# State products behind the outputs' products of the pair in front, and one place for product 7

## The chip, the cores and the metric

The kernel runs on one core of a Trainium2 chip. The metric is the device time of that core in microseconds (us), the median of several executions. A core has five engines with instruction queues of their own: TensorE (PE, the matmuls), VectorE (DVE), ScalarE (ACT), GpSimd (POOL) and SyncE (SP, which here only issues DMAs). Each runs its own queue in program order and waits for another engine through semaphores.

## The reference

Two blocks follow one another. The first is a Mamba-2 scan over 4 sequences, 8 heads, 768 tokens, head size 32, state size 16: with decays `a`, inputs `x`, and `B`, `C`, chunk by chunk

```python
M = einsum('bhin,bhjn->bhij', Cc, Bc) * exp(cum[i] - cum[j]) * causal   # gram times decays
y = einsum('bhij,bhjd->bhid', M, xc) + einsum('bhin,bhnd->bhid', Cc, state) * exp(cum)
state = exp(sum(la)) * state + sum_j(B_j * x_j * exp(cum_end - cum_j))
```

The second takes y as 3072 tokens of 256 features: `h = y @ w_in` (2048 wide), `g = max(h, 0) + alpha * min(h, 0)` (PReLU), `out = g @ w_out`. Everything is float32.

## The kernel before

**Tiles.** A chunk has 128 tokens here; a *pair* is two chunks, so there are 12 pairs, three for each sequence. A *group* is two pairs, 512 tokens, so there are 6 groups. While group g runs through the second block, the two pairs of group g + 1 are prepared by the first block. Groups 1 to 5 do the second block's two products in a Strassen-like scheme (seven products of half-size blocks in place of eight); group 0 does them directly.

**A quad.** `quad(g, z, after)` handles a quarter (z = 0 to 3) of the hidden features of a group. On TensorE it makes seven products into two banks of PSUM, A and Y, through `first` (L770). The ones that matter here, in order: `first(A, …, t3)`, `first(Y, …, b22)`, `first(A, …, t4)`, `first(Y, …, b21)`. What leaves the banks: `c22` (VectorE, L793), the copy of `m1` into Y (ScalarE, L799), and `prelu` for g12, g22, g21 and g11, each with two multiplications by ScalarE (L753) and two by VectorE (L755). g21 comes from A after `t4`, and g11 from Y after `b21`. Banks A and Y are taken from a pool with two of them (`ps_h`), which the *gram* of a pair (below) uses as well, through `spare()`.

**The order of the work** is written out by hand. `quad` calls `after(1)` to `after(14)` at fourteen places between its own steps. `after` issues there:
- `product(g, z, n)`, n = 1 to 7 (L745): the output products of the *quad in front*, by the table `with_gram` in the even quads (z = 0, 2) of groups 1 to 4, and by `without` elsewhere. The tables differ in product 7 alone: place 11 in the one, place 9 in the other. Product 6 is at place 13, product 4 at place 14.
- `ssm(gp, n)`: n further stages of the generator `pair(gp)`, by the table `steps`.
- `pair_loads(gp)` (L385, GpSimd): B times its decays, tile `bn`, which the state products read; and, in quad (3, 7), `token_sums` for the next group (L725).
- parts of `combine` and `finish`, which end the group in front, and sums of weights in group 1.

**A pair of groups 2 to 5** (pairs 4 to 11; `fine` in the code) has these stages: the transposes of B and C (L469); four stages of decays (VectorE scans, L438); the state products `added` (L519, tile shape 128x64) with the update of the state `states` (VectorE L531, GpSimd L534) and `c_decayed` (GpSimd L487); the gram `products_bc` (L569, four row groups of 32 rows each, two in tiles of `ps_s`, two in `spare()` banks, the fourth in the one that Y had) and its product with the decays (VectorE L604), in two stages; and the outputs' products (L620 from the state, shape 64x128, and L627 from the chunk, shape 128x32) with their copies to `xT` (ScalarE, L634). The state products of a pair stand in an even quad at place 9, its gram at place 13 of the same quad, its outputs' products at place 5 of the odd quad behind. The two pairs of a group take one even and one odd quad each. The last pair of each sequence (5, 8, 11) needs the state of one chunk only, so it has half the state products.

A float32 matmul shows as two TensorE instructions in the trace.

Of the kernel before, what the change touches and what calls it, by code (L numbers as in the profile page):

```python
# [9 lines left out]
F32 = mybir.dt.float32  # L10
U32 = mybir.dt.uint32
U16 = mybir.dt.uint16
ALU = mybir.AluOpType
# [9 lines left out]
def kernel(  # L23
# [25 lines left out]
    nc = tc.nc  # L49
# [6 lines left out]
    P = 128  # L56
    Q = 128
# [6 lines left out]
    KC = d_model // P  # L64
# [44 lines left out]
    def ss_tile():  # L109
        if early[0] is None:  # L110
            return ps_s.tile([P, 512], F32, name="ss")
        early[0] += 1
        i = early[0] % (3 if ident_p else 4)
        return ps_s.tile([P, 512], F32, name="ss") if i < 2 else bank(i)
# [211 lines left out]
    held = {}  # L326
    bns = {}

    def identity_bank():


        m5_bank.append(bank(3))
        nc.scalar.copy(out=m5_bank[0][:, HT:], in_=ident_h[:, :HT])
        ident_p.append(m5_bank[0][:, HT:])
# [42 lines left out]
    def pair_loads(gp):  # L377

        b, c = divmod(2 * gp, CPB)
        nat, abc, xt, ap = loads["p", gp]  # L380

        bn = work.tile([P, 2, H * N], F32, name="bn")
        i, bi = divmod(b, 2)
        pj = prt[i].rearrange("p (b h c) -> p b c h", b=2, h=H)[:, bi, c : c + 2]
        nc.gpsimd.tensor_tensor(  # L385
            out=bn.rearrange("p k (h n) -> p k h n", h=H),
            in0=nat[:, 0].rearrange("p k (h n) -> p k h n", h=H),
            in1=pj.unsqueeze(3).to_broadcast([P, 2, H, N]), op=ALU.mult)
        return bn
# [22 lines left out]
    def spare():  # L412

        return ps_h.tile([P, GT], F32, name="hp", tag="hp")

    def pair(gp):

        b, c = divmod(2 * gp, CPB)
        nat, abc, xt, ap = loads["p", gp]
        last = c + 2 == CPB  # L420
        dec = work.tile([P, 2, H, Q], F32, name="dec")
        dv = dec.rearrange("p k h t -> p k (h t)")

# [37 lines left out]
            yield  # L461


        tp = spare() if gp == 1 else ss_tile()
        if gp == 0:
            keep_warm(tp, 3, Q)
# [20 lines left out]
            nc.gpsimd.tensor_tensor(out=cd.rearrange("p k t -> p (k t)"), in0=ct, in1=pf,  # L487
                                    op=ALU.mult)

        fine = gp >= 2 * GC // 2  # L490
        if gp < 2:
            spread_c()
        if gp == 0:
# [1 line left out]
            dps = spare()  # L495
            keep_warm(dps, 6, Q)
            yield
        bn = bns.pop(gp) if gp in bns else pair_loads(gp)
        if gp == 1:
            c_decayed()  # L500
            dps = spare()
# [1 line left out]
        elif gp:  # L503
            yield

        nk = 1 if last else 2
        st = [masked.get(b)]  # L510
        new = work.tile([P, 2, P], F32, name="state")
        sm = work.tile([P, 2, P], F32, name="sm")

        def added(dps):
            dps = dps.rearrange("p (k m) -> p k m", m=P)
            for k in range(nk):
                for w in range(KC):
                    ws = slice(64 * w, 64 * w + 64)
                    nc.tensor.matmul(dps[ws, k], bn[:, k, ws], xt[:, k, w * P : (w + 1) * P],  # L519
                                     start=True, stop=True, tile_position=(0, 64 * w),  # L520
                                     skip_group_check=True)
            return dps

        def states(dps):
            for k in range(nk):
                old = state.get(b)
                if old is None:
                    nc.scalar.copy(out=new[:, k], in_=dps[:, k])
                else:
                    e = (k + 1) * Q - 1  # L530
                    nc.vector.scalar_tensor_tensor(out=new[:, k], in0=old, scalar=pf[:, e : e + 1],  # L531
                                                   in1=dps[:, k], op0=ALU.mult, op1=ALU.add)
                state[b] = new[:, k]
            nc.gpsimd.tensor_tensor(out=sm[:, :nk], in0=new[:, :nk],  # L534
                                    in1=hmask.unsqueeze(1).to_broadcast([P, nk, P]), op=ALU.mult)
            st.extend(sm[:, k] for k in range(nk))
            masked[b] = st[-1]

        if fine:
            for k in range(2):  # L540
                for w in range(2):
                    half_decays(k, w)
                    if k == 1 and w == 1:
                        spread_c()
                    yield
        else:
            if gp > 1:
                states(added(ss_tile()))
                c_decayed()
            decays(0)  # L550
            if gp == 1:
                dps = added(dps)
            if gp:
                yield
            if gp != 1:
                decays(1)
            if gp > 1:
                spread_c()
# [24 lines left out]
        if gp == 0:  # L583
            gram = products_bc()
            dps = added(dps)
            yield
            c_decayed()
            times(dec[:, :, :2], one_less(gram))
        elif gp == 1:
            decays(1)  # L590
            gram = products_bc()
            g0 = one_less(gram)
            states(dps)
            times(dec[:, :, :2], g0)
        else:
            if fine:
                states(added(ss_tile()))
                c_decayed()
            yield
            gram = products_bc()  # L600
        for i, r in enumerate(r for r in ((2, 3, 0, 1) if fine else (3, 2, 1, 0) if gp > 1 else range(4))
                              if r in gram):
# [6 lines left out]
        yield  # L609


        y = [ss_tile()[:, : 2 * Q].rearrange("p (k t) -> p k t", k=2) for w in range(KC)]
        if gp < 2:
            keep_warm(y[0].rearrange("p k t -> p (k t)"), 2 - gp)
        begun = False
# [7 lines left out]
        for k in range(2):  # L623
            for w in range(KC):
                for q in range(4):
                    h = 4 * w + q
                    nc.tensor.matmul(y[w][32 * q : 32 * q + 32, k], xt[:, k, h * D : (h + 1) * D],  # L627
                                     dec[:, k, h], start=False, stop=True,
                                     tile_position=(0, 32 * q), skip_group_check=True)
        g, q = divmod(2 * gp, GC)  # L630
        if q == 0:
            xts[g] = xtp.tile([P, KC, GT], F32, name="xT")
# [342 lines left out]
    for f in range(FIRST, NF):  # L975
        if f in (5, 10):
            load_pair(3 + f // 10)
        if f == 5:
            load_rows(1)
        hidden(0, f)  # L980
        if f <= 10:
            ssm(2)
        if f >= 9:
            ssm(3)
        if f < FIRST + 2:
            convert_a(*pieces[f + 1 + (f > FIRST)])
        convert_next(first=f > FIRST)
        if f == FIRST:
            convert_a(*pieces[6])
        if f == 8:  # L990
            bns[3] = pair_loads(3)
        if f == 8:
            rows_clamp(1)
            held["pr"] = rows_scan(1)
            rows_out(1)
        output(f - FIRST)
        if f in in_steps:
            weight_sums(wi, in_sums, 0, in_steps[f])
    early[0] = None
    token_sums(1)  # L1000
    ssm(2 * GC // 2, 2)


    steps = {(0, 1): 0, (0, 2): 0, (0, 5): 0, (0, 9): 0, (0, 13): 0, (1, 1): 0, (1, 5): 0,
             (1, 12): 1, (1, 14): 1, (2, 1): 1, (2, 2): 1, (2, 5): 1, (2, 9): 1, (2, 13): 1,
             (3, 1): 1, (3, 5): 1, (3, 12): 2, (3, 14): 2}

    late_sums = {(0, 2): ((wqt, out_sums, 0, 0),), (0, 4): ((wqt, out_sums, 0, 1),),
# [6 lines left out]
    last_out = {3: ((0, 0),), 5: ((1, 0),), 7: ((2, 0),), 8: ((3, 0),), 11: ((0, 1),), 13: ((1, 1),),  # L1015
            14: ((2, 1), (3, 1))}

    with_gram = {3: 1, 5: 2, 7: 3, 8: 5, 11: 7, 13: 6, 14: 4}
    without = {3: 1, 5: 2, 7: 3, 8: 5, 9: 7, 13: 6, 14: 4}
    for i in range(NZ * (NG - 1)):  # L1020
        g, z = divmod(NZ + i, NZ)
        nxt = 2 * g + 2

        def after(j, g=g, z=z, i=i, nxt=nxt):
            places = with_gram if nxt < NP and z % 2 == 0 else without
            if i and j in places:
                product(*divmod(NZ + i - 1, NZ), places[j])
            if i == 0:
                for f, half in last_out.get(j, ()):
                    output(NF - LATE + f, half)  # L1030
            if (i, j) in ((0, 13), (1, 8)):
                store_first(i)
            for args in late_sums.get((i, j), ()):
                weight_sums(*args)
            if g > 1 and z == 0 and j in (5, 9, 13, 14):
                if j == 5:
                    comb[0] = combine(g - 1)
                next(comb[0], None)
            if g > 1 and z in (1, 3) and j == 11:
                finish(g - 1, z // 2)  # L1040
            if nxt + steps.get((z, j), NP) < NP:
                ssm(nxt + steps[z, j])
            if nxt < NP and (z, j) == (3, 7):
                token_sums(g + 1)
            ahead = nxt + {(1, 3): 1, (3, 8): 2}.get((z, j), NP)
            if ahead < NP:
                if ahead == 6:
                    rows_turn(1, held["pr"])
                bns[ahead] = pair_loads(ahead)

        comb = [None] if i == 0 else comb
        if z == 0 and nxt < NP:
            load_pair(nxt + 1)
        if z == 2 and nxt + 2 < NP:
            load_pair(nxt + 2)
        quad(g, z, after)
# [31 lines left out]
```

## Time and profile before

| what | value |
|---|---|
| time, median of 3 runs | 374.32 us (374.3 to 375.46) |
| span of the profiled execution | 372.9 us |
| TensorE busy | 365.1 us (98%) |
| VectorE, ScalarE, GpSimd busy | 243.9, 179.4, 201.1 us |
| granted TensorE clock | 0.998 |
| matmul instructions, L745 (output products) | 560, 140.8 us |
| L770 (`first`) | 560, 146.3 us |
| L569 (gram), all | 192, 31.6 us |
| L519 (state products), all | 80, 7.0 us |
| L620 and L627 (outputs' products), all | 464, 25.3 us |

The page gives busy time for each engine, the span in slices, the chain of work that ended last, and the costliest groups of instructions, with the idle time ahead of them and the instruction that ended it. A TensorE row's length is modelled, so lengths of neighbouring rows overlap; times between the *starts* of rows are what was measured. The timeline lists rows in order of time: start, length, engine, line, operation, output and inputs, shapes, and how many like rows were merged.

### The profile page before, as it was taken

Reading aid. Unit: us, or ns where it says so; the run is one execution under the profiler, and the core shown is the slowest. Engines: PE = TensorE matmul, PEld = TensorE weight load, DVE = VectorE, ACT = ScalarE, POOL = GpSimd, SP = SyncE. Lnnn points to the kernel's source line nnn. Section 1 sums busy time; section 2 is a strip of 40 time slices with the busy share of each in tenths; the row PEclk is TensorE's granted clock in tenths of the full one; section 3 lists DMA queues with packets and bytes.
Section 4 is the critical chain, followed back from the end, with each engine's and each line's share of the span. In section 5 each row is a group of like instructions: output and inputs, shape, how many; then the busy total and the mean of one; then the engine's idle time right before and its main releaser. Section 6 shows DMA issues by size and latency. Waiting matters only on the chain.

```text
span 372.9 us, 6183 instructions
## 1 busy us (share of the span) xinstructions
PE 365.1 (98%) x2223; PEld 294.3 (79%) x2223; DVE 243.9 (65%) x462; ACT 179.4 (48%) x384; POOL 201.1 (54%) x211
## 2 busy tenths in 40 slices
PE   8899999999999999999999999999999999999996
PEld 8676666578778788788788788788788788888884
DVE  7897989976438648738638847637847644543364
ACT  2558766435255345444444445445535525553541
POOL 4876566777928744724645535555455355264512
PEclk9999999999999999999999999999999999999999
DMA  7999997901029601003703603701901001001003
GB/s 146 212 186 313 244 321 150 187 15 58 28 49 182 109 3 56 2 0 58 155 3 61 150 2 52 161 0 31 179 5 29 2 0 22 9 0 30 1 0 84
DMA packets 121878, 30.71 MB, mean 82 GB/s; under 512 B 93736, under 2 KB 117752, under 8 KB 121848
## 3 DMA queue, kind: packets, MB, share of 16 engines
q1 hardware_dynamic: 116736, 29.74, 36.0%
q10 hardware_dynamic: 5112, 0.59, 1.1%
q8 instruction: 17, 0.28, 0.3%
q14 instruction: 13, 0.11, 0.1%
HBM read 26.98 MB, written 3.34 MB: 81 GB/s over the span
## 4 chain that ended last, share of the span: by engine, by line
PE 92%; POOL 3%; DVE 2%; issue 1%; ACT 1%; POOLq 0%; DVEq 0%; ACTq 0%
PE hp L770 33%; PE bank L745 32%; PE bank L684 8%; PE hp L646 6%; PE ss L627 2%; PE ss L569 2%; PE ss L620 1%; PE ss L519 1%; PE hp L569 1%; PE ss L469 1%; PE hp L270 1%; PE bank L569 1%; POOL w_in L261 1%; POOL bn L385 1%; PE hp L661 1%
## 5 line engine op out<-in xcount | busy, mean ns | idle before, releaser
L813 POOL TENSOR_TENSOR gt<-gt 128x512 f32<-128x512 f32 x58 | 73.7, 1270 | 31.4 <-DVE gt L755 24.5
L755 DVE SCALAR_TENSOR_TENSOR gt<-hp,s_mul,gt 128x256 f32<-128x256 f32 x120 | 52.6, 480 | 47.6 <-ACT gt L753 46.3
L745 PE MATMUL bank<-gt,w_out 128*128 128x256 f32 x320 | 82.5, 382 | 0.4 <-ACT o_sb L691 0.4
L753 ACT ACTIVATE gt<-hp,s_alpha 128x256 f32<-128x256 f32 x120 | 50.3, 470 | 46.8 <-PE hp L770 32.7
L745 PEld LDWEIGHTS bank<-gt,w_out 128*128 128x128 f32 x320 | 60.0, 190 | 11.2 <-issue 2.3
L804 POOL TENSOR_TENSOR gt<-gt 128x512 f32<-128x512 f32 x20 | 25.4, 1272 | 79.1 <-DVE gt L755 79.1
L745 PE MATMUL bank<-gt,ws 128*128 128x256 f32 x240 | 58.3, 379 | 0.0
L745 PEld LDWEIGHTS bank<-gt,ws 128*128 128x128 f32 x240 | 45.1, 190 | 5.8
L438 DVE TENSOR_TENSOR_SCAN dec<-abc,bank 128x256 f32<-128x256 f32 x80 | 48.1, 662 | 0.0
L770 PE MATMUL hp<-xs,w_in 128*128 128x256 f32 x160 | 42.8, 390 | 0.0
L770 PE MATMUL hp<-xT,w_in 128*128 128x256 f32 x160 | 41.9, 384 | 0.0
L770 PE MATMUL hp<-xs,ws 128*128 128x256 f32 x160 | 41.1, 379 | 0.0
L789 DVE TENSOR_TENSOR hp<-hp,u 128x512 f32<-128x512 f32 x20 | 14.0, 700 | 39.8 <-ACT u L787 39.8
L778 ACT COPY m<-hp 128x512 f32<-128x512 f32 x20 | 11.7, 586 | 51.8 <-PE hp L770 51.8
L770 PEld LDWEIGHTS hp<-xs,w_in 128*128 128x128 f32 x160 | 28.7, 189 | 7.7 <-issue 3.0
L770 PEld LDWEIGHTS hp<-xT,w_in 128*128 128x128 f32 x160 | 29.7, 190 | 5.1 <-issue 1.2
L770 PEld LDWEIGHTS hp<-xs,ws 128*128 128x128 f32 x160 | 30.4, 190 | 4.1
L684 PE MATMUL bank<-w_out,gt 128*128 128x256 f32 x128 | 31.0, 384 | 0.0
L684 PEld LDWEIGHTS bank<-w_out,gt 128*128 128x128 f32 x128 | 23.7, 190 | 6.6 <-issue 3.7
L793 DVE TENSOR_TENSOR c<-hp,m 128x512 f32<-128x512 f32 x20 | 13.6, 682 | 19.2 <-PE hp L770 19.2
L646 PE MATMUL hp<-xT,w_in 128*128 128x512 f32 x48 | 22.8, 597 | 0.2 <-POOL w_out L261 0.2
L787 ACT COPY u<-hp 128x512 f32<-128x512 f32 x20 | 11.7, 585 | 23.0 <-PE hp L770 23.0
(156 smaller groups left out, 554.4 us busy)
## 6 DMA issues: line engine op xcount, KB each, us to landing
abc<-z SPq DMA_DIRECT2D x20, 512.0 KB, 4.9
raw<-in_moe_w_in_dram SPq DMA_DIRECT2D x8, 512.0 KB, 5.2
raw<-in_moe_w_out_dram SPq DMA_DIRECT2D x8, 512.0 KB, 6.3
xt<-in_x_dram SPq DMA_DIRECT2D x24, 128.0 KB, 3.3
out_dram<-o_sb SPq DMA_DIRECT2D x32, 64.0 KB, 1.9
nat<-in_B_dram SPq DMA_DIRECT2D x22, 64.0 KB, 2.7
nat<-in_C_dram SPq DMA_DIRECT2D x22, 64.0 KB, 2.7
ap<-pf SPq DMA_DIRECT2D x11, 128.0 KB
```

The costliest lines, as they stand in the source:

```text
L438: nc.vector.tensor_tensor_scan(out=dv[:, k, hs], data0=abc[k][:, hs], data1=ident_p[0], initial=0.0, op0=ALU.mult, op1=ALU.add)
L569: nc.tensor.matmul(gram[r][:, k].rearrange("p h t -> p (h t)"), bh[rs, k], cz[rs, :, k], start=True, stop=True, tile_position=(32 * r, 0), ...
L646: nc.tensor.matmul(hp, w_in[:, k, f * P : (f + 1) * P], xts[g][:, k], start=(k == 0), stop=(k == KC - 1))
L684: nc.tensor.matmul(pos[0][t // 2][:, t % 2], gt[:, t * Q : (t + 1) * Q], w_out[:, f], start=(f == 0 and t % 2 == 0), stop=(f == NF - 1), s ...
L745: nc.tensor.matmul(ms[g][i][:, h], w, blocks[g, z][n][:, p], start=(q == 0 and h == 0), stop=(q == NQ - 1), skip_group_check=True)
L753: nc.scalar.mul(o[:, p], h[:, p], s_alpha[:, fs[p]])
L755: nc.vector.scalar_tensor_tensor(out=o[:, p], in0=h[:, p], scalar=s_mul[:, fs[p]], in1=o[:, p], op0=ALU.mult, op1=ALU.max)
L770: nc.tensor.matmul(to[:, p], w(2 * z + p), b, start=start and p == 0, stop=True, skip_group_check=True)
L789: nc.vector.tensor_tensor(out=Y, in0=Y, in1=u2, op=ALU.add)
L793: nc.vector.tensor_tensor(out=c22, in0=A, in1=m5, op=ALU.add)
L804: nc.gpsimd.tensor_tensor(out=tc_, in0=g22, in1=g12, op=ALU.subtract)
L813: eng.tensor_tensor(out=o, in0=x0, in1=x1, op=ALU.subtract)
```

## The change

The state products of a pair leave place 9 of their even quad. They are issued at place 5 of the odd quad in front, between the outputs' products of the pair in front and the copies of these, and they write into the free half of one of the two banks that the outputs' products fill (`beside`). The outputs' stage is split in two for that (a `yield` ahead of the copies), and after each odd quad's place 5 a small loop runs the next pair's state products, the copies of the pair in front, and the next pair's state update. On TensorE two visits of small tiles become one. The first such pair, 4, has no pair in front of it here; its state products are issued with its first four stages ahead of group 1. `pair_loads` moves forward to place 9 of the even quads (and, for pair 4, into group 0), since `bn` is needed earlier. `c_decayed` moves to the last stage of the decays. With the state products gone from place 9, product 7 goes to place 9 in all quads, and one table is left.

```diff
--- before.py
+++ after.py
@@ -326,6 +326,8 @@
     held = {}
     bns = {}
 
+    beside = {}
+
     def identity_bank():
 
 
@@ -418,6 +420,7 @@
         b, c = divmod(2 * gp, CPB)
         nat, abc, xt, ap = loads["p", gp]
         last = c + 2 == CPB
+        fine = gp >= 2 * GC // 2
         dec = work.tile([P, 2, H, Q], F32, name="dec")
         dv = dec.rearrange("p k h t -> p k (h t)")
 
@@ -461,50 +464,6 @@
             yield
 
 
-        tp = spare() if gp == 1 else ss_tile()
-        if gp == 0:
-            keep_warm(tp, 3, Q)
-        for i in range(2):
-            for k in range(2):
-                nc.tensor.transpose(tp[:, (2 * i + k) * P : (2 * i + k + 1) * P], nat[:, i, k],
-                                    ident)
-        bc = work.tile([P, 4, Q], F32, name="bc")
-        nc.scalar.copy(out=bc.rearrange("p i t -> p (i t)"), in_=tp)
-        bh, ct = bc[:, :2], bc[:, 2:].rearrange("p k t -> p (k t)")
-        cz = czp.tile([P, 2, 2, Q], F32, name="cz")
-        cd = work.tile([P, 2, Q], F32, name="cd")
-
-        def spread_c():
-            for e in range(2):
-                o = cz[:, e].rearrange("p k t -> p (k t)")
-                if gp == 0 and e == 1:
-                    nc.gpsimd.tensor_scalar(out=o, in0=ct, scalar1=par[:, e : e + 1],
-                                            scalar2=None, op0=ALU.mult)
-                else:
-                    nc.scalar.mul(o, ct, par[:, e : e + 1])
-
-        def c_decayed():
-            nc.gpsimd.tensor_tensor(out=cd.rearrange("p k t -> p (k t)"), in0=ct, in1=pf,
-                                    op=ALU.mult)
-
-        fine = gp >= 2 * GC // 2
-        if gp < 2:
-            spread_c()
-        if gp == 0:
-            rows_turn(0, held.pop("pr"))
-            dps = spare()
-            keep_warm(dps, 6, Q)
-            yield
-        bn = bns.pop(gp) if gp in bns else pair_loads(gp)
-        if gp == 1:
-            c_decayed()
-            dps = spare()
-            ahead[1] = spread(z, 1, lambda w: ss_tile())
-        elif gp:
-            yield
-
-
-
 
         nk = 1 if last else 2
         st = [masked.get(b)]
@@ -512,7 +471,7 @@
         sm = work.tile([P, 2, P], F32, name="sm")
 
         def added(dps):
-            dps = dps.rearrange("p (k m) -> p k m", m=P)
+            dps = dps[:, : 2 * Q].rearrange("p (k m) -> p k m", m=P)
             for k in range(nk):
                 for w in range(KC):
                     ws = slice(64 * w, 64 * w + 64)
@@ -537,11 +496,62 @@
             masked[b] = st[-1]
 
         if fine:
+            bn = bns.pop(gp) if gp in bns else pair_loads(gp)
+            dps = added(beside.pop(gp) if gp in beside else ss_tile()[:, : 2 * Q])
+            yield
+            states(dps)
+            yield
+
+
+        tp = spare() if gp == 1 else ss_tile()
+        if gp == 0:
+            keep_warm(tp, 3, Q)
+        for i in range(2):
+            for k in range(2):
+                nc.tensor.transpose(tp[:, (2 * i + k) * P : (2 * i + k + 1) * P], nat[:, i, k],
+                                    ident)
+        bc = work.tile([P, 4, Q], F32, name="bc")
+        nc.scalar.copy(out=bc.rearrange("p i t -> p (i t)"), in_=tp)
+        bh, ct = bc[:, :2], bc[:, 2:].rearrange("p k t -> p (k t)")
+        cz = czp.tile([P, 2, 2, Q], F32, name="cz")
+        cd = work.tile([P, 2, Q], F32, name="cd")
+
+        def spread_c():
+            for e in range(2):
+                o = cz[:, e].rearrange("p k t -> p (k t)")
+                if gp == 0 and e == 1:
+                    nc.gpsimd.tensor_scalar(out=o, in0=ct, scalar1=par[:, e : e + 1],
+                                            scalar2=None, op0=ALU.mult)
+                else:
+                    nc.scalar.mul(o, ct, par[:, e : e + 1])
+
+        def c_decayed():
+            nc.gpsimd.tensor_tensor(out=cd.rearrange("p k t -> p (k t)"), in0=ct, in1=pf,
+                                    op=ALU.mult)
+
+        if gp < 2:
+            spread_c()
+        if gp == 0:
+            rows_turn(0, held.pop("pr"))
+            dps = spare()
+            keep_warm(dps, 6, Q)
+            yield
+        if not fine:
+            bn = bns.pop(gp) if gp in bns else pair_loads(gp)
+        if gp == 1:
+            c_decayed()
+            dps = spare()
+            ahead[1] = spread(z, 1, lambda w: ss_tile())
+        elif gp:
+            yield
+
+        if fine:
             for k in range(2):
                 for w in range(2):
                     half_decays(k, w)
                     if k == 1 and w == 1:
                         spread_c()
+                        c_decayed()
                     yield
         else:
             if gp > 1:
@@ -593,10 +603,8 @@
             states(dps)
             times(dec[:, :, :2], g0)
         else:
-            if fine:
-                states(added(ss_tile()))
-                c_decayed()
-            yield
+            if not fine:
+                yield
             gram = products_bc()
         for i, r in enumerate(r for r in ((2, 3, 0, 1) if fine else (3, 2, 1, 0) if gp > 1 else range(4))
                               if r in gram):
@@ -609,7 +617,10 @@
         yield
 
 
-        y = [ss_tile()[:, : 2 * Q].rearrange("p (k t) -> p k t", k=2) for w in range(KC)]
+        ys = [ss_tile() for w in range(KC)]
+        y = [t[:, : 2 * Q].rearrange("p (k t) -> p k t", k=2) for t in ys]
+        if fine:
+            beside[gp + 1] = ys[1][:, 2 * Q :]
         if gp < 2:
             keep_warm(y[0].rearrange("p k t -> p (k t)"), 2 - gp)
         begun = False
@@ -627,6 +638,8 @@
                     nc.tensor.matmul(y[w][32 * q : 32 * q + 32, k], xt[:, k, h * D : (h + 1) * D],
                                      dec[:, k, h], start=False, stop=True,
                                      tile_position=(0, 32 * q), skip_group_check=True)
+        if fine:
+            yield
         g, q = divmod(2 * gp, GC)
         if q == 0:
             xts[g] = xtp.tile([P, KC, GT], F32, name="xT")
@@ -987,6 +1000,8 @@
         convert_next(first=f > FIRST)
         if f == FIRST:
             convert_a(*pieces[6])
+        if f == 14:
+            bns[4] = pair_loads(4)
         if f == 8:
             bns[3] = pair_loads(3)
         if f == 8:
@@ -998,11 +1013,11 @@
             weight_sums(wi, in_sums, 0, in_steps[f])
     early[0] = None
     token_sums(1)
-    ssm(2 * GC // 2, 2)
-
-
-    steps = {(0, 1): 0, (0, 2): 0, (0, 5): 0, (0, 9): 0, (0, 13): 0, (1, 1): 0, (1, 5): 0,
-             (1, 12): 1, (1, 14): 1, (2, 1): 1, (2, 2): 1, (2, 5): 1, (2, 9): 1, (2, 13): 1,
+    ssm(2 * GC // 2, 4)
+
+
+    steps = {(0, 1): 0, (0, 2): 0, (0, 5): 0, (0, 13): 0, (1, 1): 0, (1, 5): 0,
+             (1, 12): 1, (1, 14): 1, (2, 1): 1, (2, 2): 1, (2, 5): 1, (2, 13): 1,
              (3, 1): 1, (3, 5): 1, (3, 12): 2, (3, 14): 2}
 
     late_sums = {(0, 2): ((wqt, out_sums, 0, 0),), (0, 4): ((wqt, out_sums, 0, 1),),
@@ -1015,14 +1030,12 @@
     last_out = {3: ((0, 0),), 5: ((1, 0),), 7: ((2, 0),), 8: ((3, 0),), 11: ((0, 1),), 13: ((1, 1),),
             14: ((2, 1), (3, 1))}
 
-    with_gram = {3: 1, 5: 2, 7: 3, 8: 5, 11: 7, 13: 6, 14: 4}
-    without = {3: 1, 5: 2, 7: 3, 8: 5, 9: 7, 13: 6, 14: 4}
+    places = {3: 1, 5: 2, 7: 3, 8: 5, 9: 7, 13: 6, 14: 4}
     for i in range(NZ * (NG - 1)):
         g, z = divmod(NZ + i, NZ)
         nxt = 2 * g + 2
 
         def after(j, g=g, z=z, i=i, nxt=nxt):
-            places = with_gram if nxt < NP and z % 2 == 0 else without
             if i and j in places:
                 product(*divmod(NZ + i - 1, NZ), places[j])
             if i == 0:
@@ -1040,9 +1053,14 @@
                 finish(g - 1, z // 2)
             if nxt + steps.get((z, j), NP) < NP:
                 ssm(nxt + steps[z, j])
+
+                if j == 5 and z % 2:
+                    for p in (1, 0, 1):
+                        if nxt + z // 2 + p < NP:
+                            ssm(nxt + z // 2 + p)
             if nxt < NP and (z, j) == (3, 7):
                 token_sums(g + 1)
-            ahead = nxt + {(1, 3): 1, (3, 8): 2}.get((z, j), NP)
+            ahead = nxt + {(0, 9): 1, (2, 9): 2}.get((z, j), NP)
             if ahead < NP:
                 if ahead == 6:
                     rows_turn(1, held["pr"])
```

More of the change, by code (lines that the diff above doesn't have):

```diff
@@ L461, in pair, with added, states @@
             yield
+        nk = 1 if last else 2
+        st = [masked.get(b)]
+        new = work.tile([P, 2, P], F32, name="state")
+        sm = work.tile([P, 2, P], F32, name="sm")
+        def added(dps):
+            dps = dps[:, : 2 * Q].rearrange("p (k m) -> p k m", m=P)
+            for k in range(nk):
+                for w in range(KC):
+                    ws = slice(64 * w, 64 * w + 64)
+                    nc.tensor.matmul(dps[ws, k], bn[:, k, ws], xt[:, k, w * P : (w + 1) * P],
+                                     start=True, stop=True, tile_position=(0, 64 * w),
+                                     skip_group_check=True)
+            return dps
+        def states(dps):
+            for k in range(nk):
+                old = state.get(b)
+                if old is None:
+                    nc.scalar.copy(out=new[:, k], in_=dps[:, k])
+                else:
+                    e = (k + 1) * Q - 1
+                    nc.vector.scalar_tensor_tensor(out=new[:, k], in0=old, scalar=pf[:, e : e + 1],
+                                                   in1=dps[:, k], op0=ALU.mult, op1=ALU.add)
+                state[b] = new[:, k]
+            nc.gpsimd.tensor_tensor(out=sm[:, :nk], in0=new[:, :nk],
+                                    in1=hmask.unsqueeze(1).to_broadcast([P, nk, P]), op=ALU.mult)
+            st.extend(sm[:, k] for k in range(nk))
+            masked[b] = st[-1]
+        if fine:
[4 more added lines that the diff above has]
+            yield
         tp = spare() if gp == 1 else ss_tile()
@@ L504, in pair @@
             yield
[L509 to L514, printed above, removed]
-            dps = dps.rearrange("p (k m) -> p k m", m=P)
[L516 to L528, printed above, removed]
-                else:
[L530 to L537, printed above, removed]
         if fine:
```

## The prediction

> **What bounds the kernel now.** I read the page first, then the chain that ended last, then TensorE's timeline in the second half and, beside it, those of VectorE and ScalarE.
>
> ```profile
> PE 365.1 (98%) x2223; PEld 294.3 (79%) x2223; DVE 243.9 (65%) x462; ACT 179.4 (48%) x384; POOL 201.1 (54%) x211
> PE 92%; POOL 3%; DVE 2%; issue 1%; ACT 1%; POOLq 0%; DVEq 0%; ACTq 0%
> ```
>
> TensorE is the bound, and almost nothing visible stops it. The change adds no matmul and takes none away, so only the cost of the *order* on TensorE can move. The timeline (columns: start, length, then the group) of one even quad, pair 7:
>
> ```profile
> 177.95 1.03 PE L770 MATMUL hp<-xs,w_in 128*128 128x256 f32 x4
> 178.91 0.66 PE L519 MATMUL ss<-xt,bn 128*64 128x128 f32 x8
> 179.50 1.13 PE L770 MATMUL hp<-xT,w_in 128*128 128x256 f32 x4
> 180.46 1.03 PE L745 MATMUL bank<-gt,w_out 128*128 128x256 f32 x4
> 181.33 1.03 PE L745 MATMUL bank<-gt,ws 128*128 128x256 f32 x4
> 182.28 0.48 PE L569 MATMUL ss<-cz,bc 32*128 32x256 f32 x2
> 182.30 0.71 PE L569 MATMUL hp<-cz,bc 32*128 32x256 f32 x2
> ...
> 183.58 1.13 PE L745 MATMUL bank<-gt,w_out 128*128 128x256 f32 x4
> ```
>
> Starts are what to read, since ends are modelled. Four full-size matmuls take 0.864 us start to start (180.46 to 181.33), 0.216 each. In order: `first(A, …, t4)`, the state products (L519), `first(Y, …, b21)`, product 7, product 6, the gram of C and B (L569), product 4. Beside it VectorE and ScalarE:
>
> ```profile
> 180.72 0.84 ACT L753 ACTIVATE gt<-hp,s_alpha 128x256 f32<-128x256 f32 x2 [0.81 <-PE hp L770]
> ```
> ```profile
> 180.74 0.72 DVE L531 SCALAR_TENSOR_TENSOR state<-state,ap,ss 128x128 f32<-128x128 f32 x2
> 181.60 0.88 DVE L755 SCALAR_TENSOR_TENSOR gt<-hp,s_mul,gt 128x256 f32<-128x256 f32 x2
> ```
>
> The L755 row is the PReLU of g11, the last reader of bank Y. It ends at 181.60 + 0.88 = 182.48. The gram's fourth row group needs the bank that Y leaves; its first matmul starts at 182.53, while the other three start at 182.28 to 182.30. So the gram is **already held** by this PReLU, by some 0.23 us. Over all eight grams of the late part, the next full-size matmul starts 1.10 to 1.12 us after that PReLU's end (183.58 − 182.48 = 1.10; pair 4: 95.74 − (93.75 + 0.87) = 1.12). I use 1.11. The list of waits (total, times, longest) names this wait only once, on the weight loads, because the modelled matmul ends cover the others:
>
> ```profile
> PEld hp L569 <- DVE gt L755: 0.3, 1, 0.3
> ```
>
> The same chain where nothing lies between, in an odd quad:
>
> ```profile
> 195.90 1.03 PE L770 MATMUL hp<-xT,w_in 128*128 128x256 f32 x4
> ```
> ```profile
> 197.90 0.88 DVE L755 SCALAR_TENSOR_TENSOR gt<-hp,s_mul,gt 128x256 f32<-128x256 f32 x2 [0.78 <-ACT gt L753]
> ```
>
> From the start of `first(Y, …, b21)` to the end of its PReLU: 197.90 + 0.88 − 195.90 = **2.88 us** (matmuls, then ScalarE twice, then VectorE twice). In the even quad it is 2.98, because the first matmul after small tiles takes 0.32 instead of 0.216. VectorE's state update at 180.74 isn't what delays it.
>
> **What the Trainium skill says.** Trainium Kernel Development and Optimization, Performance Expectations: matmul busy time is a bad measure, as matmuls are pipelined; agreed, a 0.23 us hold stands inside "98%". TensorEngine Tiling (Array Packing), Key Properties: changing the tiling mode drains TensorE. The trace agrees: each change of tile shape costs 0.309 instead of 0.216 us between starts, and the first interval behind it is longer (0.32 for full-size ones). TensorE: Matmul & The Clock Gate, The mechanism: matmuls start in program order. The trace agrees where it matters: in pair 4's gram, whose fourth row group is late by 0.56 us, the second chunk's matmuls come behind it.
>
> **The change, part by part.**
>
> *State products taken out of the even quads.* Their visit costs, for eight matmuls, 0.309 (in) + 0.385 (first to last) + 0.202 (out) + 0.32 (first full-size one) − 2 × 0.216 = 0.78 us; 0.57 for four (pairs 5, 8, 11, the last pair of a sequence).
>
> *State products put behind the outputs' products of the pair in front* (seven times, pairs 5 to 11). The outputs' visit now ends with 0.203 us into full-size matmuls; instead it has one more change of shape (the one between its own two shapes, L620 to L627, takes 0.202), then 0.385 and 0.202 out. Added: 0.202 + 0.385 + 0.202 − 0.203 = 0.586 us for eight, with 0.167 for four 0.368. If this change of shape needed no drain, it would be 0.14 less; I take the full price. So merging alone saves 0.2 us a pair.
>
> *Product 7 moved from place 11 to place 9 in even quads.* It fills the hole the state products leave, but it was also what stood between `first(Y, …, b21)` and the gram. Behind `first(Y)` there is now only product 6: TensorE reaches the gram 0.864 + 0.864 + 0.093 = 1.82 us after the start of `first(Y)`, while the bank comes free at 2.88 + 0.05. So **the gram waits about 1.1 us**, and product 4 and the next quad queue behind it. From `first(A, …, t4)` to the matmul after the gram:
> - after: 8 × 0.216 + 2.88 + 1.11 = 5.72 us
> - before, eight matmuls (pairs 6, 7, 9, 10): 183.58 − 177.95 = 5.63; four (pairs 5, 8, 11): 5.41, 5.50, 5.41
>
> So the even quad loses the whole state visit and gets no shorter: +0.09 × 4, and +0.31, +0.22, +0.31: +1.20 us. With the merged visits 4 × 0.586 + 3 × 0.368 = 3.45, pairs 5 to 11 add **4.65 us**.
>
> *Pair 4* has no pair in front. Its products go ahead of its transposes at 81.36: 0.093 + 0.385 + 0.202, and some 0.05 for the first transpose's longer interval (an estimate, from the state products' own first interval of 0.16 instead of 0.107) = +0.73. In quad (1, 0) no product 7 exists, but halves of the first outputs stand there. There the gram hangs on VectorE (PReLU, state update, a subtraction, PReLU); without the 0.72 us state update only some 0.47 comes back, as the PReLU then waits for ScalarE. Net **+0.26**.
>
> *The earlier bn, state update and masking; c_decayed earlier; copies later.* Costed at nothing. bn of the next pair (0.65 us on GpSimd) moves to place 9, behind a subtraction ending at 266.7 in the tightest group, while its B, issued by 262.9, takes 2.7 to land (the page's DMA rows), to 265.6. For pair 4 it follows the conversion ending at 80.0, before 81.4. The copies (0.65) and state update (0.72) in odd quads stay off the path: VectorE is idle for 2.26 us ahead of c22 there, and ScalarE's copy of m1 into Y, the end of that chain, is done at 194.59 + 0.59 = 195.18, 0.7 us before `first(Y, …, b21)` at 195.90. The token sums (2.9 us, starting at 190.98) are needed only after 199, so half a microsecond of delay is hidden. The turn of the second rows moves from one place to another at the same price.
>
> Sum: 4.65 + 0.26 = 4.9 us; 374.32 + 4.9 = **379.2 us**.
>
> **Rivals.**
> - *Faster: the gram doesn't wait.* Then only merging counts: 7 × 0.2 = 1.4 us, less pair 4: about 373. For it: the page shows hardly any wait on TensorE. Against: the constant 1.11 us behind the PReLU in eight grams, and 2.88 us of chain against 1.82 us of cover. 0.10.
> - *Half the wait.* If ScalarE and VectorE ran the two halves of g11 overlapped once VectorE is freer, the chain would be about 0.4 us shorter: 7 × 0.4 = 2.8 less, 376.4; and near no change if the cheap switch came on top. Against: in the odd quad VectorE is free and yet starts only behind both of ScalarE's. 0.12, a third of it within 0.3%.
> - *Worse: the odd quads wait too.* State update ahead of c22, or copies held by the state products, so that `first(Y)` waits 0.4 us in seven odd quads: 382. Against: the slack above. 0.08.
>
> **How the numbers follow.** The forecast has 0.70 and its terms reach from 378.2 (the drainless switch, 7 × 0.14) to 380.2 (pair 4 getting nothing back, small delays). The range 376.9 to 380.8 takes in part of the half-wait case and leaves out the faster one and most of the worst. Faster 0.10, within 0.3% 0.04, slower 0.86.
>
> **What would show it.** In even quads: L770 x4, L745 x4 (product 7), L770, L745 (product 6), L569, and the fourth row group's first matmul about 1.1 us behind the other three; `first(A)` to the matmul after the gram 5.7 us; VectorE's first L604 beginning only behind it. In odd quads: L620, L627, L519 in one row, 2.24 us from the first L620 (eight of L620, eight of L519) to the next L770, where it is 1.66 now (188.96 to 190.62). A waits list still nearly empty, or one with "DVE gt L755" ahead of L569. Wrong, if the fourth row group starts with the others: then bank Y wasn't what held it.

## The result, and the profile after

| | before | after |
|---|---|---|
| time, median | 374.31 us | 379.76 us |
| ratio, after to before | | 1.0139, 95% interval 1.0116 to 1.0163 |
| span of the profiled execution | 372.9 us | 377.8 us |

The change makes the kernel 5.4 us slower, where 4.9 were forecast. (The median before is that of four runs here, of three in the table further up.) The page's first row and the chain that ended last, after the change:

```profile
PE 367.1 (97%) x2223; PEld 294.9 (78%) x2223; DVE 246.6 (65%) x462; ACT 180.3 (48%) x384; POOL 201.2 (53%) x211
PE 88%; DVE 4%; POOL 3%; ACT 3%; issue 1%; POOLq 0%; ACTq 0%; DVEq 0%
```

The matmuls are the same 2223. TensorE's busy time grew by only 2 us of the 4.9 of the span, and its share fell by one point. The chain tells more: 4 points of it have gone from PE to DVE and ACT, which had 2% and 1% of it before. The list of waits on TensorE (total, times, longest) has a new first line:

```profile
PE hp L579 <- DVE gt L768: 3.0, 8, 0.4
```

L579 is the gram (L569 before), L768 VectorE's half of the PReLU (L755 before). Eight grams wait. The list counts 0.4 us at most for one, since it measures from the modelled ends of the matmuls ahead of them. The timeline of TensorE shows the starts, here for the even quad of pair 7:

```profile
180.21 1.03 PE L783 MATMUL hp<-xs,w_in 128*128 128x256 f32 x4
181.07 1.03 PE L758 MATMUL bank<-gt,w_out 128*128 128x256 f32 x4
181.93 1.03 PE L783 MATMUL hp<-xT,w_in 128*128 128x256 f32 x4
182.80 1.03 PE L758 MATMUL bank<-gt,ws 128*128 128x256 f32 x4
183.75 0.48 PE L579 MATMUL ss<-cz,bc 32*128 32x256 f32 x2
183.77 0.48 PE L579 MATMUL hp<-cz,bc 32*128 32x256 f32 x1
...
184.86 0.48 PE L579 MATMUL hp<-cz,bc 32*128 32x256 f32 x1 [0.40 <-DVE gt L768]
...
185.92 0.92 PE L758 MATMUL bank<-gt,w_out 128*128 128x256 f32 x3
```

And VectorE in the same stretch:

```profile
183.93 0.88 DVE L768 SCALAR_TENSOR_TENSOR gt<-hp,s_mul,gt 128x256 f32<-128x256 f32 x2 [0.85 <-ACT gt L766]
185.64 0.69 DVE L612 TENSOR_TENSOR dec<-hp,dec 128x512 f32<-128x512 f32 x1 [0.84 <-PE hp L579]
```

(The last row of either view is cut at the edge of the window.) Read from the top: t4, product 7, b21, product 6, and the gram at 183.75. Three row groups start by 183.77, the fourth at 184.86, 1.09 us later and 0.05 us behind the PReLU's end (183.93 + 0.88 = 184.81). The PReLU ends 2.88 us after b21 starts. The next full-size matmul comes 1.11 us after the PReLU, and t4 to that matmul is 5.71 us.

The odd quad behind it shows the merged visit, here with the four state products of pair 8:

```profile
191.29 0.72 PE L631 MATMUL ss<-cd,sm 64*128 64x128 f32 x8
191.94 1.08 PE L638 MATMUL ss<-dec,xt 128*32 128x128 f32 x32
192.95 0.44 PE L478 MATMUL ss<-xt,bn 128*64 128x128 f32 x4
193.32 1.13 PE L783 MATMUL hp<-xs,w_in 128*128 128x256 f32 x4
```

The whole difference can be laid out quad by quad (first matmul of a quad to that of the next, in us; quad (group, z); worked out from the starts in the trace):

| quad | before | after | difference | product 7 at 11 again (first experiment), to before |
|---|---|---|---|---|
| (1,0) | 15.77 | 15.50 | −0.27 | −0.27 |
| (1,1) | 15.09 | 15.46 | +0.37 | +0.37 |
| (1,2) | 14.29 | 14.70 | +0.41 | −0.37 |
| (1,3) | 14.49 | 14.97 | +0.47 | +0.47 |
| (2,0) | 14.51 | 14.59 | +0.08 | −0.49 |
| (2,1) | 14.16 | 14.74 | +0.59 | +0.59 |
| (2,2) | 14.45 | 14.53 | +0.08 | −0.54 |
| (2,3) | 14.38 | 14.75 | +0.37 | +0.37 |
| (3,0) | 14.38 | 14.59 | +0.22 | −0.35 |
| (3,1) | 14.38 | 14.97 | +0.59 | +0.59 |
| (3,2) | 14.45 | 14.53 | +0.08 | −0.54 |
| (3,3) | 14.16 | 14.74 | +0.59 | +0.59 |
| (4,0) | 14.51 | 14.59 | +0.08 | −0.49 |
| (4,1) | 14.38 | 14.75 | +0.37 | +0.37 |
| (4,2) | 14.23 | 14.53 | +0.30 | −0.32 |
| (4,3) and group 5 | | | 0.00 | 0.00 |

From (1,1) to (4,2) the change adds 4.59 us: 3.35 in the odd quads, which got the state products, and 1.25 in the even quads, which lost them. The even quads are the surprise: by the prediction's prices the visit that left them was worth 4 × 0.78 + 3 × 0.57 = 4.8 us, and they got longer all the same.

### The profile page after: what moved, and what is told of

It is laid out like the page before. It is cut to its first block, busy times and chain, and to the rows that moved or that the text cites. A ratio compares the mean times of both kernels' runs of the same rounds, so it can differ in the third digit from the quotient of the medians.

```text
span 377.8 us, 6171 instructions
## 1 busy us (share of the span) xinstructions
PE 367.1 (97%) x2223; PEld 294.9 (78%) x2223; DVE 246.6 (65%) x462; ACT 180.3 (48%) x384; POOL 201.2 (53%) x211
## 3 DMA queue, kind: packets, MB, share of 16 engines
HBM read 26.98 MB, written 3.34 MB: 80 GB/s over the span
## 4 chain that ended last, share of the span: by engine, by line
PE 88%; DVE 4%; POOL 3%; ACT 3%; issue 1%; POOLq 0%; ACTq 0%; DVEq 0%
PE hp L783 32%; PE bank L758 30%; PE bank L697 7%; PE hp L659 6%; PE ss L638 2%; PE hp L579 2%; DVE gt L768 2%; ACT gt L766 2%; PE ss L631 1%; PE ss L478 1%; PE ss L511 1%; PE hp L270 1%; PE bank L579 1%; POOL w_in L261 1%; POOL bn L387 1%
## 5 line engine op out<-in xcount | busy, mean ns | idle before, releaser
L768 DVE SCALAR_TENSOR_TENSOR gt<-hp,s_mul,gt 128x256 f32<-128x256 f32 x120 | 52.5, 479 | 49.3 <-ACT gt L766 48.5
L493 POOL TENSOR_TENSOR sm<-state,bmask 128x256 f32<-128x256 f32 (+1 forms) x12 | 7.6, 637 | 34.5 <-DVE state L490 34.4
```

The lines of the kernel that those rows point to most:

```text
L768: nc.vector.scalar_tensor_tensor(out=o[:, p], in0=h[:, p], scalar=s_mul[:, fs[p]], in1=o[:, p], op0=ALU.mult, op1=ALU.max)
```

## The experiments

The theory under test: the gram waits for the PReLU of g11, since product 7 no longer stands between b21 and the gram. Its main rival: the merged visit costs the time, by what it holds up in the odd quads. The first four kernels ran beside the kernel before at 374.47 us, the other four beside it at 374.93 us.

**1. The changed kernel, product 7 at place 11 again.**

```diff
-    places = {3: 1, 5: 2, 7: 3, 8: 5, 9: 7, 13: 6, 14: 4}
+    with_gram = {3: 1, 5: 2, 7: 3, 8: 5, 11: 7, 13: 6, 14: 4}
+    without = {3: 1, 5: 2, 7: 3, 8: 5, 9: 7, 13: 6, 14: 4}
...
         def after(j, g=g, z=z, i=i, nxt=nxt):
+            places = with_gram if nxt < NP and z % 2 == 0 else without
```

> The changed kernel with product 7 back at place 11 in the even quads of groups 1 to 4, all else as changed. Theory (the gram waits for the PReLU that reads bank Y, because product 7 no longer stands in front of it): the first matmul of t4 to the matmul after the gram is 1.0 + 2.88 + 1.11 = 5.0 us instead of 5.72 in seven quads, so 379.8 - 7 x 0.75 = 374.5 us, about as fast as the kernel before, and the fourth row group starts some 0.2 us behind the others. First rival (the state products behind the outputs' products cost the time, by holding the copies and the work on VectorE in the odd quads): stays at 379 or above. Second rival (half and half): 377.

Measured: 375.29 us, ratio to before 1.0026 (1.0013 to 1.0038). Some 80% of the loss is gone with the one line, and the rivals fall: the odd quads keep their 3.34 us, but the even ones go from +1.25 to −3.10. The even quad of pair 7 in the timeline:

```profile
178.59 1.03 PE L783 MATMUL hp<-xs,w_in 128*128 128x256 f32 x4
179.59 1.13 PE L783 MATMUL hp<-xT,w_in 128*128 128x256 f32 x4
180.56 1.03 PE L758 MATMUL bank<-gt,w_out 128*128 128x256 f32 x4
...
183.68 1.13 PE L758 MATMUL bank<-gt,w_out 128*128 128x256 f32 x4
```

t4 to the matmul behind the gram is 183.68 − 178.59 = 5.09 us, not quite the 5.0 expected: b21 starts 1.00 us after t4 instead of 0.86, right behind ScalarE's copy of m1 into Y (178.94 + 0.59 = 179.53), and its four matmuls then take 0.97 us instead of 0.86. What remains to the kernel before, 0.8 us, is for the most part two things: the last column of the table sums from (1,1) to (4,2) to +0.24 us, and pair 4 costs 0.47 (0.74 ahead of group 1, less 0.27 in quad (1,0)). So the merged visit, which takes fewer changes of shape, gains *nothing* here.

**2. The kernel before, product 7 at place 9 in all quads.**

```diff
-            places = with_gram if nxt < NP and z % 2 == 0 else without
+            places = without
```

> The kernel before with product 7 at place 9 in all quads and nothing else of the change. Theory: the even quads pay the whole visit of the state products and the gram waits as well: T, the start of b21, comes 0.864 later, the gram hangs on T + 2.98 + 1.11, so +0.87 us in each of seven quads, 374.3 + 6.1 = 380.4 us, slower than the changed kernel. Rival (the merged visit costs the time): 374.3, no change.

Measured: 380.81 us, ratio 1.0157 (1.0130 to 1.0183). Seven even quads grew by 0.78 to 0.87 us, every odd one by 0.00. In one of them the same picture as after the change, with the state products still in place:

```profile
181.09 0.66 PE L519 MATMUL ss<-xt,bn 128*64 128x128 f32 x8
181.67 1.13 PE L770 MATMUL hp<-xT,w_in 128*128 128x256 f32 x4
182.64 1.03 PE L745 MATMUL bank<-gt,ws 128*128 128x256 f32 x4
183.60 0.48 PE L569 MATMUL ss<-cz,bc 32*128 32x256 f32 x2
...
184.70 0.48 PE L569 MATMUL hp<-cz,bc 32*128 32x256 f32 x1 [0.40 <-DVE gt L755]
```

Moving product 7 alone costs 5.97 us by the quads, more than the whole change with its 5.1 (4.59 and pair 4's 0.47); the intervals of the two medians overlap.

**3 and 4. VectorE's half of that PReLU left out, in both kernels.** In the even quads of groups 1 to 4, g11 is then only h times alpha.

```diff
-        prelu(g11, Y, z, 0)
+        prelu(g11, Y, z, 0, (nc.scalar,) if g < NG - 1 and z % 2 == 0 else (nc.scalar, nc.vector))
```

> The changed kernel with VectorE's half of the PReLU of g11 left out in the even quads of groups 1 to 4, so g11 there is only h times alpha; a cut of the suspected chain by 0.88 us. Theory: the gram's fourth row group follows ScalarE's last multiplication instead, 0.9 us sooner in eight quads, 379.8 - 7.1 = 372.7 us. First rival (the merged visit): 379.8 or slightly less, since VectorE is not the bound. Second rival (bank Y is held by something else than VectorE): 379.8.

> The kernel before with the same half of the PReLU of g11 left out in the same quads (g11 there is only h times alpha). Theory: here the gram waits only 0.23 us in seven quads and 0.5 in pair 4's, so the same cut brings only 2.1 us, 372.2 us, and with the cut in both kernels the change costs 0.5 us or nothing instead of 5.4. First rival (the merged visit costs 5 us by itself): 374.3 here, and a difference of 5 us to the changed kernel with the same cut remains.

Measured: 372.00 us from the changed kernel, ratio 0.9925 (0.9901 to 0.9950), and 372.52 us from the kernel before, 0.9932 (0.9908 to 0.9957). The same cut of 0.88 us in eight quads is worth 7.8 us in one kernel and 2.0 us in the other, and with it the intervals of the two kernels overlap. In the changed kernel with the cut, t4 to the matmul behind the gram is 4.79 us:

```profile
178.34 1.03 PE L783 MATMUL hp<-xs,w_in 128*128 128x256 f32 x4
...
183.13 1.13 PE L758 MATMUL bank<-gt,w_out 128*128 128x256 f32 x4
```

So the last reader of bank Y is what the gram waited for, in both. In the kernel before nothing is left of the wait: the fourth row group starts with the others. In the changed one it still starts some 0.18 us behind them, now right behind ScalarE's half of the PReLU.

**5. The kernel before, the next pair's transposes between b21 and the gram.** If the gram of the kernel before already waits, work put there is free.

```diff
-    steps = {(0, 1): 0, (0, 2): 0, (0, 5): 0, (0, 9): 0, (0, 13): 0, (1, 1): 0, (1, 5): 0,
-             (1, 12): 1, (1, 14): 1, (2, 1): 1, (2, 2): 1, (2, 5): 1, (2, 9): 1, (2, 13): 1,
-             (3, 1): 1, (3, 5): 1, (3, 12): 2, (3, 14): 2}
+    steps = {(0, 1): 0, (0, 2): 0, (0, 5): 0, (0, 9): 0, (0, 12): 1, (0, 13): 0, (1, 1): 0,
+             (1, 5): 0, (1, 14): 1, (2, 1): 1, (2, 2): 1, (2, 5): 1, (2, 9): 1, (2, 12): 2,
+             (2, 13): 1, (3, 1): 1, (3, 5): 1, (3, 14): 2}
...
-            ahead = nxt + {(1, 3): 1, (3, 8): 2}.get((z, j), NP)
+            ahead = nxt + {(0, 9): 1, (2, 9): 2}.get((z, j), NP)
```

> The kernel before with only the transposes of the next pair moved from place 12 of the odd quads to place 12 of the even quads, between b21 and the gram (and bn made at place 9 of the even quads, as in the changed kernel). Theory: the 0.44 us of transposes there cover the 0.23 us that the gram waits for bank Y anyway, so about 0.2 us in seven quads and 0.3 in pair 4's come free: 374.4 - 1.8 = 372.6 us. Rival (TensorE's work is merely moved, nothing was waiting): 374.4, no change.

Measured: 372.66 us, ratio 0.9938 (0.9925 to 0.9952), faster than both kernels. The median is 2.3 us below that of the kernel before beside it; the quads add up to 1.8 us, the sum expected. In most pairs the transposes cost the even quad 0.22 us and save the odd one 0.44 (in quad (1,0) they cost nothing):

```profile
180.69 0.60 PE L469 MATMUL ss<-ident,nat 128*128 128x128 f32 x4
181.13 1.03 PE L745 MATMUL bank<-gt,ws 128*128 128x256 f32 x4
182.09 0.48 PE L569 MATMUL ss<-cz,bc 32*128 32x256 f32 x2
182.10 0.48 PE L569 MATMUL hp<-cz,bc 32*128 32x256 f32 x2
...
183.16 1.13 PE L745 MATMUL bank<-gt,w_out 128*128 128x256 f32 x4
```

All four row groups start together now, and the gram takes 1.07 us to the next full-size matmul instead of 1.30.

**6, 7 and 8. The changed kernel with its waits covered.** On top of the first experiment the transposes become the first stage of a pair, ahead of the state products, and stand in the even quads; in 6 in two halves (B at place 10, C at 12), in 7 all at 12. 8 is 6 with VectorE's quarter of the weight sums in quad (1, 0) behind the PReLU.

```diff
-        if fine:
-            bn = bns.pop(gp) if gp in bns else pair_loads(gp)
-            dps = added(beside.pop(gp) if gp in beside else ss_tile()[:, : 2 * Q])
-            yield
-            states(dps)
-            yield
...
+            if fine and i == 0:
+                yield
...
         if fine:
+            bn = bns.pop(gp) if gp in bns else pair_loads(gp)
+            dps = added(beside.pop(gp) if gp in beside else ss_tile()[:, : 2 * Q])
+            yield
+            states(dps)
+            yield
             for k in range(2):
...
-    ssm(2 * GC // 2, 4)
+    ssm(2 * GC // 2, 5)
...
-    steps = {(0, 1): 0, (0, 2): 0, (0, 5): 0, (0, 13): 0, (1, 1): 0, (1, 5): 0,
-             (1, 12): 1, (1, 14): 1, (2, 1): 1, (2, 2): 1, (2, 5): 1, (2, 13): 1,
-             (3, 1): 1, (3, 5): 1, (3, 12): 2, (3, 14): 2}
+    steps = {(0, 1): 0, (0, 2): 0, (0, 5): 0, (0, 10): 1, (0, 12): 1, (0, 13): 0, (1, 1): 0,
+             (1, 5): 0, (1, 14): 1, (2, 1): 1, (2, 2): 1, (2, 5): 1, (2, 10): 2, (2, 12): 2,
+             (2, 13): 1, (3, 1): 1, (3, 5): 1, (3, 14): 2}
```

This is 6 against the first experiment (the first added `yield` stands between the transposes of B and of C). 7 has no such `yield` and no entries for place 10. 8 adds to 6:

```diff
-                 (0, 10): ((wqt, out_sums, 0, 3, nc.vector),), (1, 2): ((wi, in_sums, 4, 1),),
+                 (0, 11): ((wqt, out_sums, 0, 3, nc.vector),), (1, 2): ((wi, in_sums, 4, 1),),
```

> The changed kernel with product 7 back at place 11, and with the next pair's transposes moved into the even quads, those of B at place 10 ahead of b21 and those of C at place 12 ahead of the gram (0.22 us each). Theory: the state products of the kernel before had covered two waits, the one of b21 for the copy of m1 into Y (some 0.2 us) and the gram's; with both covered again the merged visit shows what it is worth: t4 to the matmul after the gram 5.1 us, the odd quads 0.15 us longer than before, 374.4 - 2.9 + 0.1 = 371.6 us, faster than both. Rival (merging is worth nothing by itself): 373 to 374.4.

> As the one with the split, but all of the transposes at place 12 of the even quads. Theory: the gram waits no more, b21 still waits some 0.2 us: 374.4 - 1.3 = 373.1 us, between the split and the kernel with product 7 at 11 alone. Rival (one cover is as good as two): equal to the split.

> As the one with the split, and VectorE's quarter of the weight sums in quad (1, 0) moved from place 10 to place 11, behind the PReLU of g11 instead of ahead of it. Theory: pair 4's gram there waits for that PReLU behind the sum (0.68 us); 0.4 us less than the split, 371.2 us, all of it in quad (1, 0). Rival: the PReLU waits for ScalarE there as well, no change.

Measured: 6: 372.82 us, 0.9946 (0.9930 to 0.9962); 7: 373.76 us, 0.9970 (0.9956 to 0.9985); 8: 372.18 us, 0.9934 (0.9915 to 0.9952). The order of the three is the one expected, by the quads as well, though the intervals of neighbours overlap. Beside the kernel before, 6 gains 2.1 us where 2.8 were expected; 0.4 of the rest is pair 4, where the visit ahead of group 1 (+0.68) and quad (1, 0) (−0.22) come to 0.5 us and not to the 0.1 set down. In an even quad of 6, b21 follows the first transposes without a gap and the four row groups start together:

```profile
177.46 1.03 PE L782 MATMUL hp<-xs,w_in 128*128 128x256 f32 x4
178.32 0.38 PE L503 MATMUL ss<-ident,nat 128*128 128x128 f32 x2
178.54 1.05 PE L782 MATMUL hp<-xT,w_in 128*128 128x256 f32 x4
...
181.47 0.48 PE L578 MATMUL ss<-cz,bc 32*128 32x256 f32 x2
181.48 0.49 PE L578 MATMUL hp<-cz,bc 32*128 32x256 f32 x2
...
182.55 0.70 PE L757 MATMUL bank<-gt,w_out 128*128 128x256 f32 x2
```

t4 to the matmul behind the gram is 5.09 us, as in the first experiment, but with the 0.44 us of transposes inside. In pair 7, (2,1) of 6 is 0.15 us longer than before and (2,2) 0.54 shorter: 0.39 us gained, against 0.22 in experiment 5, which keeps the two visits apart. From (1,1) to (4,2) 6 gains 2.57 us and 5 gains 1.81, so the merged visit is worth 0.11 us a pair on average, and 0.20 in the best pair, once the gap it leaves is filled. Pair 4 takes 0.46 us of the difference back, and the median of 6 is no lower than that of 5. In 8 quad (1, 0) is 0.77 us shorter than before, which pays for pair 4's visit. Summed over the quads and that visit, 8 is 2.7 us ahead of the kernel before and 5 is 1.8; the two medians lie 0.5 us apart, and their intervals don't tell them apart. Both beat both kernels.

## Why the prediction was right

- **The gram's wait.** Forecast from b21 to the PReLU 2.88 us, from there to the next full-size matmul 1.11, t4 to that matmul 5.72. Measured 2.88, 1.11 and 5.71. The seven even quads: +1.20 forecast, +1.25 measured; experiments 1 to 4 show the cause by taking it away, by bringing it into the kernel before, and by cutting the reader of the bank.
- **The merged visits.** +0.586 and +0.368 forecast, 0.59 and 0.37 measured; the change from tile shape 128x32 to 128x64 takes 0.202 us between starts, as the one from 64x128 to 128x32 does, so the full price was the right one. The one odd quad with +0.47 lost the turn of the second rows, which moved into (1,2); the sum over the two is the forecast's.
- **Costed at nothing.** The copies and the state update in the odd quads. One copy does wait for the state products, and the state update for that copy, as was thought possible:

```profile
192.87 0.37 ACT L647 COPY xT<-ss 128x256 f32<-128x256 f32 x1 [1.75 <-PE ss L638]
193.44 0.37 ACT L647 COPY xT<-ss 128x256 f32<-128x256 f32 x1 [0.20 <-PE ss L478]
```
```profile
193.84 0.35 DVE L490 SCALAR_TENSOR_TENSOR state<-state,ap,ss 128x128 f32<-128x128 f32 x1 [1.99 <-ACT xT L647]
194.49 0.69 DVE L806 TENSOR_TENSOR c<-hp,m 128x512 f32<-128x512 f32 x1 [0.30 <-PE hp L783]
```

  c22 (L806) still waits for its matmuls, so nothing is lost; the odd quads grew by the visit and by no more.
- **Pair 4.** +0.73 forecast for the visit ahead of group 1; 0.74 measured (the last outputs' group of four times two matmuls to the first quad: 2.91 us after, 2.17 before). Of the 0.47 that was to come back in quad (1, 0), only 0.27 did. This term was mis-sized: the PReLU was said to wait for ScalarE there, but it still waited for VectorE's own weight sum, which took 1.05 us in place of 0.68. Experiment 8, which moves that sum behind the PReLU, makes the quad 0.55 us shorter than in experiment 6.
- **"Merging alone saves 0.2 us a pair"** was right as a count of TensorE's changes of shape, and wrong as the gain of the rival case without the gram's wait, set at 373: experiment 1 brings the gram's wait back to the 0.23 us of before and isn't faster than before. Where they stood, the state products had covered the wait of b21 for bank Y (for the copy of m1), which the prediction's sum for that rival leaves out. In experiment 1 b21 starts 0.14 us late in pair 7 and its matmuls take 0.11 longer, which together eat the 0.2. The gram's wait they had not covered, though the expectation of experiment 6 says so: it is 0.23 us with them and without them, and product 7 is what covers the rest of it.
- The sum, 4.65 + 0.26 = 4.9 us, against 4.59 + 0.47 = 5.1 from the quads with pair 4's visit, and 5.4 in the medians. The remaining 0.3 us isn't explained; the stretch ahead of group 1 scatters by more than that from one profiled execution to another: with its code unchanged, the first quad of group 1 starts at 80.1 to 80.9 us after the first matmul in four traces of kernels made from the one before.

## What to carry to other kernels

On an engine that is always busy, a piece of work has two values: its own time, and the wait of the next instruction that it covers. Before moving it, find the instruction behind the gap, who frees its buffer, and how long that chain is from its first matmul; if the work left in the gap is shorter than the chain, moving costs the difference. Read it from the starts of the rows: a constant distance between another engine's last reader and the next matmul, over many repetitions, shows a wait that the busy share hid here and the list of waits named once for eight. Where such a wait is found, other work can be moved *into* it: that is what gained time in experiments 5 to 8.

## What the runs showed of the hardware

VectorE's sum of two operands in SBUF (quarter 3 of the weight sums) took 0.68 us in the kernels built on the one before and 0.99 to 1.05 us in all those of the changed order, until experiment 8 moved it. Where it was long, a bn product on GpSimd had started 0.14 to 0.20 us ahead of it. Where it was short in the old order, GpSimd's masking of the state began 0.23 us after it, and took 1.04 us in place of 0.73. The Trainium skill, SBUF — State Buffer, Who interferes with whom, says that a VectorE instruction with two inputs in SBUF and a GpSimd instruction that reads SBUF exclude each other, and that the later one blocks. These lengths agree on which of the two grows, in both orders; the growth of 0.31 to 0.37 us is some 0.14 us less than what the earlier one still had to run (0.45 to 0.50). The earlier pair_loads of the change is not enough to make VectorE the later one: experiment 5 has it too, but with the masking still ahead of it, and the sum took 0.68 us. No run isolates it further.
